# The seam between the mlp and attention: four copy buffers, passing products, bank sets by order of release, and a first turn without row maxima

## The chip, the cores and the metric

The kernel runs on one core of a Trainium2 chip. The metric is device time in microseconds (us). TensorE (PE) multiplies, VectorE (DVE), ScalarE (ACT) and GpSimd (POOL) work element by element, SyncE (SP) issues most of the transfers.

## The reference

Input x is 2048 x 448, all in float32. Two branches are mixed by a gate per token:

```
g = sigmoid((x * gate_w).sum(-1))
a = softmax(q k^T * 28**-0.5) v  per head (16 heads of 28), then @ wo      # q, k, v = x @ wqkv
b = gelu(layernorm(x) @ w1 + b1) @ w2 + b2                                   # 448 -> 1792 -> 448
out = g * a + (1 - g) * b
```

## The kernel before

Each float32 factor is split into a high part (rounded to fp32r, the matmul's one-pass type) and a low part (the rest), and a product is made of three: high by high, high by low, low by high.

The work has two stages. In the first (class `Strips`), PE is used as four strips of 32 rows; each strip has its own stream of small matmuls. A planner in Python (`Strips.run`, with estimated costs and ready times) writes their order out: first q, k and v (`QK`, `Val`), then the mlp in four chunks of 512 tokens: 14 tiles of w1 with the gelu (`Up`), then four tiles of w2 (`Down`, one of 128 tokens each). A piece collects in one of the PSUM banks 0 to 5; when its last strip is done, `close` empties the bank. For `Down` that is a copy by ACT into a buffer `gb` (L381, L382; two buffers) and a DMA issued from ACT's own queue to `gbs` in DRAM (L385). `st.free[bank]` holds the planner's estimate of the time at which a bank comes free.

Between these pieces, in both stages, run the row maxima of attention: a product of 128 queries with 512 keys in high precision only (L199), and a reduction on DVE (L201). 1024 of them are needed in all, kept in banks 6 and 7 in the first stage. Their results, by way of DRAM (`ms`), become a 29th row of the queries, so that the exp needs no further shift. They must be ready before the 64 units of a chunk that uses them.

The second stage is attention. Its unit is one head's 128 keys by 512 queries; there are 1024 units, 64 to each pair of a head group and a chunk of queries. A turn (`turn_of`) makes the scores of five units while row maxima are owed, and of six later. The turn's first three units go to banks 0, 1, 2 and the other two or three to banks 3, 4 (5): three passes of products each (L1108), then one exp of ACT over the bank set (L1111, tiles `p0` and `p1`). Turns of five units slip in three row maxima (`lone`), by way of banks 6, 5 and 6, turns of six up to two. Behind the scores stand the products of probabilities and values for all units of earlier turns, four at a time (`batch`, L1119, bank 7). In turn 0 there are none yet, and six products of the keys with themselves, whose result nobody reads, stand in their place (L1135, bank 7).

PE's order is exactly the order of the code. ACT, DVE, POOL and SP have each their own stream, in the order of the code; semaphores join the streams.

At the seam, the last four `Down` tiles (chunk 3) lie in banks 5, 1, 3 and 0, and are closed in that order. Attention's first scores, of turn 0, follow them on PE, with one maximum ahead of them. These scores need banks 0, 1 and 2.

Of the kernel before, what the change touches and what calls it, by code (L numbers as in the profile page):

```python
# [7 lines left out]
F32 = mybir.dt.float32  # L8
F32R = mybir.dt.float32r
AF = mybir.ActivationFunctionType  # L10
# [5 lines left out]
P = 128  # L16
S = 2048
D = 448
# [4 lines left out]
CH = 512  # L23
NC = S // CH
# [5 lines left out]
SCALE = DH ** -0.5  # L30
# [5 lines left out]
def kernel(ctx: ExitStack, tc: tile.TileContext, xt, wqk, wv, wo, xk, w1, b1, w2, b2,  # L36
                          ident_d, sel_d, out):
    nc = tc.nc
# [35 lines left out]
    bk = banks.tile([P, 8, CH], F32, name="bk")  # L74
# [87 lines left out]
    class RowMax:  # L162
# [51 lines left out]
        def close(self, n):  # L214
            mf, mt = self.mf[n % 2], self.mt[n % 2]
            nc.vector.reduce_max(mf[:, 0:16], self.mx[n % 2].rearrange("p j i k -> p (j i) k"), axis=AX)
            nc.vector.transpose(mt, mf)
# [17 lines left out]
    mhp = []  # L235
# [120 lines left out]
    class Down(Piece):  # L356
# [21 lines left out]
            return st.hready.get((self.c, f, p), 1e9) > now or self.c == 0 and st.w2ready.get(f, 1e9) > now  # L378

        def close(self, st, now):  # L380
            gb = mhp[0].tile([P, D], F32, name="gb", bufs=2)  # L381
            nc.scalar.activation(gb, bk[:, self.bank, :D], AF.Copy)  # L382
            st.use("act", now + 0.2, 0.56)
            st.free[self.bank] = st.act + 0.1
            nc.scalar.dma_start(gbs[self.c * TPC + self.i], gb)  # L385
            st.use("act", now, 0.5)

    class Strips:
# [28 lines left out]
        def at(self, t, fn, **uses):  # L417
            self.tasks.append((t, self.count, fn, uses))
            self.count += 1
# [358 lines left out]
    khi, klo, vg = {}, {}, {}  # L778
# [73 lines left out]
    strips = Strips([])  # L852
# [3 lines left out]
    for i, key in enumerate(load):  # L856
        r = slots[i % 8]
# [43 lines left out]
    m1.close()  # L901
    loads[0] = nc.sync


    def sb(name, bufs):
        return ctx.enter_context(tc.tile_pool(name=name, bufs=bufs, reuse_waits="tile"))
# [45 lines left out]
    def products(po, tt, groups):  # L952
        c, i = divmod(tt, TPC)
        sl = slice(i * P, (i + 1) * P)
        for g in groups:
            h, l = (t[:, g, sl] for t in ohs[c])
            nc.tensor.matmul(po, h, woh[:, g], start=(g == 0), stop=False, skip_group_check=True)  # L957
            nc.tensor.matmul(po, h, wol[:, g], start=False, stop=False, skip_group_check=True)  # L958
            nc.tensor.matmul(po, l, woh[:, g], start=False, stop=(g == NG - 1), skip_group_check=True)  # L959
# [7 lines left out]
    def project(tt):  # L967
        po = bk[:, 6, :D]
        products(po, tt, range(NG))
        put(po, tt)  # L970
# [60 lines left out]
    def begun(n, turn):  # L1031

        g, c = divmod(n, NC)
        if n + 1 < NG * NC:
            for j in range(4):
                at(turn + 1 + j // 2, lambda j=j: fetch_qq(n + 1, j))
            at(turn + 5, lambda: split_qq(n + 1))
            at(turn + 7, lambda: load_ms(n + 1))
        if c == (0 if g == 0 else 2) and g < NG - 1:
            for j in range(4):  # L1040
                at(turn + 2 + j, lambda j=j: fetch_kk(g + 1, j))
                at(turn + 8 + j, lambda j=j: split_kk(g + 1, j))
            at(turn + 13, lambda: key_row(g + 1))
            for t in range(2):
                at(turn + 9 + t, lambda t=t: load_v(g + 1, slice(8 * t, 8 * t + 8)))
        if g == NG - 1:
            for i in range(TPC):
                at(turn + 7 + i, lambda i=i: fetch_acc(c, i))
                at(turn + 9 + i // 2, lambda i=i: weigh_acc(c, i))
            for x in range(NG - 1):  # L1050
                at(turn + 4 + x, lambda x=x: split_o(x, c, ot[x][:, c * CH:(c + 1) * CH]))
# [14 lines left out]
    UNITS = NG * NC * 64  # L1066
    prob, tail = {}, []
    begins = set()
    cold = [0] * 4

    def lone(s, b, turn):
        if not rowmax.ready(s) or turn < cold[s]:
            return
        for kind, n, j in rowmax.one(s, bk[:, b]):
            if kind == "q":
                at(turn + 1, lambda n=n, j=j: rowmax.load_q(n, j))
            elif kind == "k":
                at(turn + 1, lambda n=n, j=j: rowmax.load_k(n, j))
                cold[j] = turn + 4
            else:  # L1080
                at(turn + 1, lambda n=n: rowmax.close(n))
                at(turn + 2, lambda n=n: rowmax.store(n))

    def turn_of(u, turn):

        left = UNITS - u
        owed = rowmax.left()
        size = min(left, 5 if owed and owed > 2 * ((left - 116) // 6) else 6)
        na, nb = min(3, size), max(0, size - 3)
        for x in range(u, u + size):  # L1090
            n = x // 64
            if n not in begins:
                begins.add(n)
                begun(n, turn)
        extra = {5: ((0, 3, 6), (3, 1, 5), (5, 2, 6)), 6: ((0, 3, 6), (5, 2, 6))}.get(size, ())
        for half, first, count in ((0, 0, na), (1, 3, nb)):
            for p in range(3):
                for x, o, b in extra:
                    if x == 3 * half + p:
                        lone((u + o) % 4, b, turn)  # L1100
                for i in range(first, first + count):
                    n, k = divmod(u + i, 64)
                    k, j = divmod(k, 4)
                    r = slice(32 * j, 32 * j + DH + (p == 0))
                    ks = slice(k * P, (k + 1) * P)
                    w = (khi, klo, khi)[p][n // NC]
                    q = (qh, qh, ql)[p][n % 3]
                    nc.tensor.matmul(bk[:, i], w[r, ks], q[r], start=(p == 0), stop=(p == 2), skip_group_check=True)  # L1108
            if count:
                t = ap.tile([P, 3, CH], F32, name=f"p{half}")  # L1110
                nc.scalar.activation(t[:, :count], bk[:, first:first + count], AF.Exp, scale=SCALE)  # L1111
                for i in range(count):
                    prob[u + first + i] = t[:, i]
        return size

    def batch(b, turn):
        n, k = divmod(b, NT)
        for j in range(4):
            nc.tensor.matmul(bk[32 * j:32 * j + 32, 7], vg[n // NC][:, k, 32 * j:32 * j + 32], prob.pop(4 * b + j),  # L1119
                             start=(k == 0), stop=(k == NT - 1), skip_group_check=True)  # L1120
        if k == NT - 1:
            valued(n, turn)
            return True
        return False

    u = b = turn = 0
    while b < UNITS // 4:
        before = u
        if u < UNITS:
            u += turn_of(u, turn)  # L1130
        for fn in agenda.pop(turn, ()):
            fn()
        if turn == 0:
            for _ in range(6):
                nc.tensor.matmul(bk[:, 7], khi[0][:, 0:P], khi[0][:, 0:CH], start=True, stop=True)  # L1135
        if before == UNITS:
            products(bk[:, 6, :D], (NC - 1) * TPC, range(NG - 1))
            before = u = UNITS
        while 4 * b + 4 <= before:
            b += 1  # L1140
            if batch(b - 1, turn):
                break
        if tail and tail[0][0] <= turn:
            project(tail.pop(0)[1])
        turn += 1
# [53 lines left out]
```

## Time and profile before

| | us |
|---|---|
| median of three runs | 1098.76 (1096.95 to 1099.1) |
| the profiled execution | 1098.27 |
| its span, first to last instruction | 1096.2 |
| PE busy | 1078.5 (98%) |
| DVE, ACT, POOL busy | 740.3, 634.5, 363.5 |
| mean granted clock of TensorE | 0.995 |

The page gives busy time and instructions of each engine; the span in 40 slices (the digits are tenths of busy time, for PEclk tenths of the full clock); the chain of work that ended last; and groups of instructions by line. In a timeline a row is: start, duration, engine, line, operation, what it writes and reads, how many; in brackets the idle time of the engine ahead of it and what ended that. "ACTq" and "SPq" are the issue of a DMA by that engine. A table of windows gives for each stretch its length, the busy time of each engine with its instructions in brackets, the granted clock, and the DMA engines' share and rate. In the chain of waits a row is start, duration and what.

### The profile page before, as it was taken

What the parts mean: (1) busy time and instruction counts of PE and PEld (TensorE: products, weight loads), DVE (VectorE), ACT (ScalarE), POOL (GpSimd) and SP (SyncE); (2) the same over time, 40 slices, a digit from 0 to 9 for tenths busy, and PEclk for the clock granted to TensorE, in tenths of its full rate; (3) what the DMA queues carried; (4) which work ended last, traced back from release to release, by engine and by line L of the source; (5) the groups of instructions that cost most, each with busy time, mean ns of one, the idle gap of its engine ahead of it and who ended that gap; (6) DMA issues with size and microseconds to landing.
All of it is one profiled execution on the core that took longest, in us unless ns stands there. A gap on an engine that the chain in (4) does not pass through costs nothing.

```text
span 1096.2 us, 30487 instructions
## 1 busy us (share of the span) xinstructions
PE 1078.5 (98%) x13166; PEld 726.3 (66%) x13166; DVE 740.3 (68%) x1186; ACT 634.5 (58%) x668; POOL 363.5 (33%) x372
## 2 busy tenths in 40 slices
PE   9999999999999999999999999999999999999998
PEld 7999999999999989544444444444444444454555
DVE  4289889999999998667766766567667666320102
ACT  5334471141250250478878878878878878857671
POOL 3547687245152166501100100310011215245431
PEclk9999999999999999899999999999999999999999
DMA  6795543104100105501000000500002101011111
GB/s 230 215 312 185 167 123 97 42 4 103 40 7 11 41 8 126 149 9 27 18 17 16 23 23 17 125 16 14 20 21 63 45 16 54 25 51 38 60 53 59
DMA packets 47462, 73.15 MB, mean 67 GB/s; under 512 B 13632, under 2 KB 28608, under 8 KB 46416
## 3 DMA queue, kind: packets, MB, share of 16 engines
q1 hardware_dynamic: 33888, 39.11, 12.9%
q0 software_dynamic: 4800, 16.89, 5.3%
q10 hardware_dynamic: 8640, 15.21, 3.9%
q8 instruction: 103, 1.69, 0.6%
q14 instruction: 31, 0.25, 0.1%
HBM read 51.75 MB, written 19.31 MB: 65 GB/s over the span
## 4 chain that ended last, share of the span: by engine, by line
PE 92%; ACT 3%; DVE 2%; issue 1%; DMA 1%; POOL 0%; SPq 0%; DVEq 0%; ACTq 0%; POOLq 0%
PE bk L472 33%; PE bk L1119 22%; PE bk L1108 18%; PE bk L199 15%; ACT p L1111 2%; PE bk L957 1%; PE bk L958 1%; PE bk L959 1%; DVE mx L201 1%; PE bk L883 1%; DMA first<-in_xt 0%; DMA gbs<-gb 0%; PE bk L1135 0%; ACT gb L382 0%; POOL hl L350 0%
## 5 line engine op out<-in xcount | busy, mean ns | idle before, releaser
L201 DVE TENSOR_REDUCE mx<-bk 128x1 f32<-128x512 f32 x1024 | 672.1, 688 | 203.7 <-PE bk L199 164.7
L1111 ACT ACTIVATE p<-bk 128x1536 f32<-128x1536 f32 (+1 forms) x395 | 481.7, 1275 | 147.4 <-PE bk L1108 147.4
L199 PE MATMUL bk<-kd,qd 28*128 28x512 f32 x1024 | 446.7, 439 | 3.3 <-DVE mx L201 1.8
L199 PEld LDWEIGHTS bk<-kd,qd 28*128 28x128 f32 x1024 | 186.4, 182 | 197.0 <-DVE mx L201 130.5
L472 PE MATMUL bk<-yh,w1f 32*128 32x512 f32 x1568 | 183.4, 392 | 0.4 <-ACT gb L382 0.4
L472 PE MATMUL bk<-yl,w1f 32*128 32x512 f32 x784 | 161.0, 391 | 0.0
L472 PEld LDWEIGHTS bk<-yh,w1f 32*128 32x128 f32 x1568 | 150.8, 183 | 2.3 <-ACT gb L382 1.7
L472 PE MATMUL bk<-w2h,hh 32*128 32x448 f32 x896 | 133.2, 366 | 1.3 <-ACT hh L343 1.3
L472 PE MATMUL bk<-w2l,hh 32*128 32x448 f32 x896 | 132.5, 363 | 0.0
L1119 PE MATMUL bk<-p,va 128*32 128x512 f32 x1024 | 132.1, 606 | 0.0
L1119 PE MATMUL bk<-p,vb 128*32 128x512 f32 x1024 | 129.5, 601 | 0.0
L350 POOL TENSOR_TENSOR hl<-h,hh 128x512 fp32r<-128x512 f32 x56 | 73.6, 1324 | 131.6 <-ACT hh L343 71.1
L1108 PE MATMUL bk<-yh,ka 29*128 29x512 f32 x512 | 108.4, 487 | 1.8 <-ACT gb L382 1.8
L803 POOL CAST yh<-yl 128x512 fp32r<-128x512 f32 x16 | 9.8, 610 | 298.0 <-DMA yl<-qk 219.6
L472 PEld LDWEIGHTS bk<-yl,w1f 32*128 32x128 f32 x784 | 103.3, 183 | 0.2
L1108 PE MATMUL bk<-yh,kb 29*128 29x512 f32 x512 | 98.4, 477 | 3.7 <-ACT p L1111 3.7
L472 PEld LDWEIGHTS bk<-w2h,hh 32*128 32x128 f32 x896 | 99.1, 183 | 1.8 <-ACT hh L343 1.7
L472 PEld LDWEIGHTS bk<-w2l,hh 32*128 32x128 f32 x896 | 99.9, 183 | 0.2
L1108 PE MATMUL bk<-yh,la 28*128 28x512 f32 x512 | 90.0, 397 | 0.0
L382 ACT ACTIVATE gb<-bk 128x448 f32<-128x448 f32 x16 | 8.7, 544 | 139.0 <-PE bk L472 134.2
L1108 PE MATMUL bk<-yl,ka 28*128 28x512 f32 x512 | 88.7, 413 | 0.0
L472 PE MATMUL bk<-w2h,hl 32*128 32x448 f32 x896 | 87.5, 362 | 0.0
(140 smaller groups left out, 1595.1 us busy)
## 6 DMA issues: line engine op xcount, KB each, us to landing
qk<-qo ACTq DMA_DIRECT2D x28, 256.0 KB
raw<-in_xt SPq DMA_DIRECT2D x17, 256.0 KB
vs<-vt ACTq DMA_DIRECT2D x16, 256.0 KB
rc<-rls SPq DMA_DIRECT2D x60, 64.0 KB
bxr<-in_xk POOLq DMA_DIRECT2D x8, 448.0 KB, 6.2
gbs<-gb ACTq DMA_DIRECT2D x16, 224.0 KB
acc<-gbs SPq DMA_DIRECT2D x16, 224.0 KB
out_y<-acc SPq DMA_DIRECT2D x16, 224.0 KB
```

The lines of the kernel that those rows point to most:

```text
L199: nc.tensor.matmul(ps, self.qd[n % 2][r, i * P:(i + 1) * P], self.kd[r, k * 512:(k + 1) * 512], start=True, stop=True)
L201: nc.vector.reduce_max(self.mx[n % 2][:, j, i, k:k + 1], ps, axis=AX)
L350: nc.gpsimd.tensor_sub(hl[f], h, hh[f].bitcast(F32))
L472: mm = nc.tensor.matmul(bk[:, x.bank, :n], a, b, start=x.first, stop=(len(x.rem) == 1 and m == len(ops) - 1), skip_group_check=True)
L803: nc.gpsimd.tensor_copy(h, l.bitcast(F32))
L883: nc.tensor.matmul(bk[:, b], w, v, start=(i == 0), stop=(i == len(ops) - 1), skip_group_check=True)
L957: nc.tensor.matmul(po, h, woh[:, g], start=(g == 0), stop=False, skip_group_check=True)
L958: nc.tensor.matmul(po, h, wol[:, g], start=False, stop=False, skip_group_check=True)
L959: nc.tensor.matmul(po, l, woh[:, g], start=False, stop=(g == NG - 1), skip_group_check=True)
L1108: nc.tensor.matmul(bk[:, i], w[r, ks], q[r], start=(p == 0), stop=(p == 2), skip_group_check=True)
L1111: nc.scalar.activation(t[:, :count], bk[:, first:first + count], AF.Exp, scale=SCALE)
L1119: nc.tensor.matmul(bk[32 * j:32 * j + 32, 7], vg[n // NC][:, k, 32 * j:32 * j + 32], prob.pop(4 * b + j), start=(k == 0), stop=(k == NT - ...
```

## The change

Four edits at the seam:

- The third and fourth of the last four `Down` tiles are copied to two buffers of the name `h` (those of the gelu, last used by the mlp's last `Up` tiles) instead of waiting for the two of `gb`.
- `shift` chooses, by the planner's estimates, which half of the banks 0 to 5 is free first; turns then use the sets in that order (`turn_bank`). Here the first set becomes banks 3, 4, 5 and the second 0, 1, 2, for all turns. The maxima that went to bank 5 go to bank 2.
- `idle` writes four products of the keys with themselves (nobody reads them) into the bank that has been free longest, bank 2, between the last mlp product and the first scores. The six of turn 0 stay.
- `cold = [1] * 4`: turn 0 makes no row maxima.

```diff
         def close(self, st, now):
-            gb = mhp[0].tile([P, D], F32, name="gb", bufs=2)
+            if self.c == NC - 1 and self.i > 1:
+                gb = mhp[0].tile([P, CH], F32, name="h", bufs=2)[:, :D]
+            else:
+                gb = mhp[0].tile([P, D], F32, name="gb", bufs=2)
             nc.scalar.activation(gb, bk[:, self.bank, :D], AF.Copy)
...
+    shift = min((0, 3), key=lambda o: max(strips.free[o + i] for i in range(3)))
+
+    def turn_bank(i):
+        return (i + shift) % 6
+
+    def idle(n, b):
+        for _ in range(n):
+            nc.tensor.matmul(bk[:, b], khi[0][:, 0:P], khi[0][:, 0:CH], start=True, stop=True)
+
+    idle(4, min(range(6), key=lambda b: strips.free[b]))
...
-    cold = [0] * 4
+    cold = [1] * 4
...
-                        lone((u + o) % 4, b, turn)
+                        lone((u + o) % 4, b if b == 6 else turn_bank(b), turn)
...
-                    nc.tensor.matmul(bk[:, i], w[r, ks], q[r], start=(p == 0), stop=(p == 2), skip_group_check=True)
+                    nc.tensor.matmul(bk[:, turn_bank(i)], w[r, ks], q[r], start=(p == 0), stop=(p == 2), skip_group_check=True)
...
-                nc.scalar.activation(t[:, :count], bk[:, first:first + count], AF.Exp, scale=SCALE)
+                b = turn_bank(first)
+                nc.scalar.activation(t[:, :count], bk[:, b:b + count], AF.Exp, scale=SCALE)
...
         if turn == 0:
-            for _ in range(6):
-                nc.tensor.matmul(bk[:, 7], khi[0][:, 0:P], khi[0][:, 0:CH], start=True, stop=True)
+            idle(6, 7)
```

What the change moves is seen in the order of the instructions. On PE, before the change, from the last `Down` products (L472) over turn 0 to the start of turn 1:

```order
L199 MATMUL bk<-kd,qd_150 128x512
L472 MATMUL bk<-w2h_3668,hl_2824 128x448
L199 MATMUL bk<-kd,qd_150 128x512
L1108 MATMUL bk<-yh,ka 128x512 x3
L1108 MATMUL bk<-yh,la 128x512 x3
L1108 MATMUL bk<-yl,ka 128x512 x3
L199 MATMUL bk<-kd,qd_150 128x512
L1108 MATMUL bk<-yh,ka 128x512 x2
L1108 MATMUL bk<-yh,la 128x512 x2
L199 MATMUL bk<-kd,qd_150 128x512
L1108 MATMUL bk<-yl,ka 128x512 x2
L1135 MATMUL bk<-ka 128x512 x6
```

The same place on PE after the change (its lines are 3 to 14 higher; L1121 is the scores, L914 the products of `idle`):

```order
L199 MATMUL bk<-kd,qd_150 128x512
L475 MATMUL bk<-w2h_3668,hl_2824 128x448
L914 MATMUL bk<-ka 128x512 x4
L1121 MATMUL bk<-yh,ka 128x512 x3
L1121 MATMUL bk<-yh,la 128x512 x3
L1121 MATMUL bk<-yl,ka 128x512 x3
L1121 MATMUL bk<-yh,ka 128x512 x2
L1121 MATMUL bk<-yh,la 128x512 x2
L1121 MATMUL bk<-yl,ka 128x512 x2
L914 MATMUL bk<-ka 128x512 x6
```

The four passing products took the place of turn 0's first maximum, and the two others are gone from between the scores. On ACT, before the change, the last four copies of `Down` with their DMA issues, and the first exps:

```order
L382 ACTIVATE gb_9624<-bk_115 128x448
L385 DMA gbs_90<-gb_9624 128x448
L382 ACTIVATE gb_9630<-bk_115 128x448
L385 DMA gbs_90<-gb_9630 128x448
L382 ACTIVATE gb_9639<-bk_115 128x448
L385 DMA gbs_90<-gb_9639 128x448
L382 ACTIVATE gb_9647<-bk_115 128x448
L385 DMA gbs_90<-gb_9647 128x448
L1111 ACTIVATE p0_9677<-bk_115 128x1536
```

And after it:

```order
L385 ACTIVATE gb_9624<-bk_115 128x448
L388 DMA gbs_90<-gb_9624 128x448
L385 ACTIVATE gb_9630<-bk_115 128x448
L388 DMA gbs_90<-gb_9630 128x448
L385 ACTIVATE h_9639<-bk_115 128x448
L388 DMA gbs_90<-h_9639 128x448
L385 ACTIVATE h_9647<-bk_115 128x448
L388 DMA gbs_90<-h_9647 128x448
L1125 ACTIVATE p0_9679<-bk_115 128x1536
```

The order is the same; only the third and fourth copy write another buffer. Since turn 0 makes no maxima, the later turns make them: before, 159 turns have five units, 38 have six, and the last has one; after, 161 have five, 36 have six, and the last has three. The number of turns stays 198.

## The prediction

> **What bounds the kernel now.** I read the page's busy shares first, then its row of the granted TensorE clock, then the chain.
>
> ```profile
> PE 1078.5 (98%) x13166; PEld 726.3 (66%) x13166; DVE 740.3 (68%) x1186; ACT 634.5 (58%) x668; POOL 363.5 (33%) x372
> ...
> PEclk9999999999999999899999999999999999999999
> ...
> PE bk L472 33%; PE bk L1119 22%; PE bk L1108 18%; PE bk L199 15%; ACT p L1111 2%; PE bk L957 1%; PE bk L958 1%; PE bk L959 1%; DVE mx L201 1%; PE bk L883 1%; DMA first<-in_xt 0%; DMA gbs<-gb 0%; PE bk L1135 0%; ACT gb L382 0%; POOL hl L350 0%
> ```
>
> TensorE is the bound: 1078.5 of 1096.2 us busy, and it fills the chain. So a gain must come from a stretch in which PE idles or runs slowly. The clock row has one dip, in the slice around 450 us, exactly where the mlp's last tiles give way to attention's first scores. I then cut that stretch into windows of 3.41 us, with one earlier thin window beside them.
>
> ```profile
> core 0: us, PE busy (x) PEld busy (x) DVE busy (x) ACT busy (x) POOL busy (x), PEclk, DMA share, GB/s
> 405.33:408.75 3.42, 2.10 (x43) 1.61 (x39) 2.38 (x4) 1.72 (x4) 3.12 (x3) 1.00 0.01 2
> 442.88:446.29 3.41, 2.85 (x44) 2.23 (x36) 3.34 (x6) 1.09 (x2) 1.73 (x3) 1.00 0.25 96
> 446.29:449.71 3.42, 1.44 (x16) 1.14 (x17) 0.87 (x2) 1.09 (x2) 1.58 (x2) 1.00 0.62 206
> 449.71:453.12 3.41, 3.41 (x14) 2.17 (x8) 1.29 (x2) 2.37 (x2) 0.00 (x0) 0.50 0.73 218
> 453.12:456.53 3.41, 3.41 (x21) 1.91 (x20) 1.44 (x3) 1.16 (x1) 2.34 (x4) 0.50 0.88 226
> 456.53:459.95 3.42, 3.42 (x23) 1.47 (x23) 1.23 (x2) 1.20 (x2) 3.34 (x4) 0.50 0.18 44
> 459.95:463.36 3.41, 3.41 (x36) 1.69 (x30) 2.43 (x4) 2.98 (x3) 3.25 (x5) 1.00 1.08 286
> ```
>
> The reader is to see two losses in one place. From 446.29 to 449.71 PE works only 1.44 of 3.42 us, 42%. Straight after it the granted clock is 0.50 for three windows, 10.24 us, although PE's rows are full; that is at most 10.24 x 0.5 = 5.1 us of lost PE time. A window with 2.10 of 3.42 us busy, 61%, at 405.33 drew no such answer. So the dip is bought somewhere between 42% and 61% of work in a window. The timeline shows why PE stood.
>
> ```profile
> 444.53 0.54 ACT L382 ACTIVATE gb<-bk 128x448 f32<-128x448 f32 x1 [34.39 <-PE bk L472]
> 445.11 0.33 ACTq L385 DMA_DIRECT2D gbs<-gb  x1
> ...
> 445.31 0.40 PE L472 MATMUL bk<-w2h,hl 32*128 32x448 f32 x1
> 445.54 0.54 ACT L382 ACTIVATE gb<-bk 128x448 f32<-128x448 f32 x1 [0.46 <-PE bk L472]
> 446.11 0.33 ACTq L385 DMA_DIRECT2D gbs<-gb  x1
> ...
> 446.52 0.50 PE L199 MATMUL bk<-kd,qd 28*128 28x512 f32 x1 [0.78 <-DVE mx L201]
> ...
> 447.13 0.54 ACT L382 ACTIVATE gb<-bk 128x448 f32<-128x448 f32 x1 [1.05 <-DMA gbs<-gb]
> 447.70 0.33 ACTq L385 DMA_DIRECT2D gbs<-gb  x1
> 448.13 0.54 ACT L382 ACTIVATE gb<-bk 128x448 f32<-128x448 f32 x1 [0.46 <-DMA gbs<-gb]
> 448.70 0.33 ACTq L385 DMA_DIRECT2D gbs<-gb  x1
> ...
> 448.77 0.65 PE L1108 MATMUL bk<-yh,ka 29*128 29x512 f32 x4 [1.75 <-ACT gb L382]
> ...
> 449.08 0.58 PE L1108 MATMUL bk<-yh,la 28*128 28x512 f32 x4
> ...
> 449.31 0.63 PE L1108 MATMUL bk<-yl,ka 28*128 28x512 f32 x4
> ```
>
> The last mlp product ends at 445.71. The third copy waits for a buffer (releaser: the DMA of the first copy). The first scores go to banks 0 to 2, bank 0 is emptied by the fourth copy, and PE starts them 0.10 us after that one's end (448.67 to 448.77). Each round of scores follows the one before by 0.23 us (449.08 to 449.31).
>
> **The change, part by part.** *Four buffers.* A copy follows the DMA issue ahead of it by 0.43 us when nothing is waited for (445.11 to 445.54). So copy three starts at 446.11 + 0.43 = 446.54 instead of 447.13 and ends at 447.08; its DMA is issued at 447.11, and copy four runs from 447.54 to 448.08, with its DMA issue at 448.11. The new buffers were last read by POOL's low parts (L350); the row of POOL is idle for 13.42 us until 444.48, so they are free.
>
> ```profile
> 444.48 0.56 POOL L928 CAST woh<-ob 128x448 fp32r<-128x448 f32 x1 [13.42 <-PE bk L472]
> ```
>
> *Bank sets.* The first set is now banks 3 to 5, whose last occupant is copy three; scores start at 447.08 + 0.10 = 447.18, which is 1.59 us sooner. The second half's banks wait for copy four, to 448.18, about when the first half's nine products have been issued.
>
> *Passing products.* Four full-height products go to an unused bank right behind the last mlp product, from about 445.55. A price is read from the six that stand there already, at half clock:
>
> ```profile
> 450.81 2.93 PE L1135 MATMUL bk<-ka 128*128 128x512 f32 x6
> ...
> 453.67 0.79 PE L199 MATMUL bk<-kd,qd 28*128 28x512 f32 x1
> ```
>
> That is 0.49 us each, 0.24 at full clock: four end near 446.5, before the scores may start. Their cover is the wait for copy three; without it they would cost 1.0 us. The idle stretch shrinks from 2.6 us (0.81 + 1.75, around the lone L199) to about 0.7, and the window from 446.29 to 449.71 then holds about 2.7 of 3.4 us, 80%, above the 61% that passed. **I take the clock to stay at 1.00.**
>
> Here a rule can be weighed. The Trainium skill, "TensorE: Matmul & The Clock Gate", section "Why this matters for your kernels", says to avoid idle gaps above about 3 us between bursts. By it the gaps here (0.81 and 1.75 us) are harmless, the dip has another cause and stays, and the change brings 1.6 us alone; that ends where the first rival below does. The trace disagrees so far, with 0.50 granted right behind the thin window. The same page, section "What's actually happening", has one busy window of about 3.4 us bring the clock back; by it a dip would cost 1.7 us, as the second rival's shortest does, but here three windows of full PE rows passed first.
>
> *The first turn without maxima.* Turn 0 has nine scores, then six; at full clock the first exp follows the first score by 1.04 us (448.77 to 449.81, below). So it is ready at 448.22, but ScalarE is free only 0.43 us after its last DMA issue: 448.54. It ends at 449.99. The second half's six scores run two side by side, three rounds of 0.23 us, 448.18 to about 448.9; six passing products follow to 448.9 + 6 x 0.24 = 450.3. Turn 1 starts there instead of at 453.67, and banks 3 to 5 are free. Its exp starts at 450.3 + 1.05 = 451.35. From there I go by the exps:
>
> ```profile
> 449.81 2.37 ACT L1111 ACTIVATE p<-bk 128x1536 f32<-128x1536 f32 x2 [1.14 <-PE bk L1108]
> 455.37 2.37 ACT L1111 ACTIVATE p<-bk 128x1536 f32<-128x1536 f32 x2 [3.19 <-PE bk L1108]
> 460.09 2.37 ACT L1111 ACTIVATE p<-bk 128x1536 f32<-128x1536 f32 x2 [2.35 <-PE bk L1108]
> 462.74 2.37 ACT L1111 ACTIVATE p<-bk 128x1536 f32<-128x1536 f32 x2 [0.29 <-PE bk L1108]
> 465.50 2.37 ACT L1111 ACTIVATE p<-bk 128x1536 f32<-128x1536 f32 x2 [0.38 <-PE bk L1108]
> 469.06 2.37 ACT L1111 ACTIVATE p<-bk 128x1536 f32<-128x1536 f32 x2 [1.20 <-PE bk L1108]
> ```
>
> Before, turns 0, 1, 2 are 5.56 and 4.72 us apart, then 2.65, 2.76, 3.56 (the last with two batches of value products). Now turns 1 to 5 come at 451.35, 454.06 (taking 2.71 for a turn with one batch), 456.7, 459.5 and 463.06. **The gain at turn 5 is 469.06 - 463.06 = 6.0 us.** It lies between 1.59 (clock drops all the same) and 1.59 + 5.1 = 6.7 (every half-speed microsecond was pure loss).
>
> *The three deferred maxima.* They are spread over later turns. By the order, turns stay 198, but 161 instead of 159 have five units, and the last turn has three instead of one. Rows for what this is worth:
>
> ```profile
> 466.19 1.85 PE bk L1119 x16
> 477.87 1.86 PE bk L1119 x16
> ...
> 1045.08 1.85 PE bk L1119 x16
> ...
> 1051.75 1.86 PE bk L1119 x16
> ```
>
> Four turns of five units take 11.68 us, a pair 5.84 with 2.5 batches; a pair of sixes takes 6.67 with three, so 6.67 - 0.46 (half a batch; sixteen rows are two batches in 1.85) = 6.21 against 5.84. Two sixes that become fives save at most 0.4 us. Against it stand three maxima of 0.23 us, 0.7 us if nothing ran beside them. Between -0.4 and +0.7 I take 0, since each shares PE with scores on other rows of the array. The last turn's exp grows from 0.60 us to the 1.45 of three banks:
>
> ```profile
> 1077.22 0.60 ACT L1111 ACTIVATE p<-bk 128x512 f32<-128x512 f32 x1 [3.26 <-PE bk L1108]
> ...
> 1080.08 1.06 PE L1119 MATMUL bk<-p,vb 128*32 128x512 f32 x8
> ```
>
> Its user starts at 1080.08 and 1077.22 + 1.45 = 1078.67, so it stays covered, with 1.4 us to spare.
>
> The profiled execution took 1098.27 us, 2.1 of them outside its span. **1098.27 - 6.0 = 1092.3 us.** That execution is 0.5 us under the median of the three runs, 1098.76; they spread by 2.1.
>
> **The rivals.** *The clock drops anyway* (passing products and strips of 28 rows may count for less than their rows suggest): only the earlier start stays, 1098.27 - 1.59 = 1096.7. The same time follows if the dip has another cause than the thin window. For it: PE's rows were full in the dip and the clock still took three windows. Against it: the window at 405.33, of row strips alone, passed at 61%.
>
> *A shorter dip*: one or two half-speed windows, 1.7 us each, give 1094.0 or 1095.7.
>
> *Slower: the clock drops and stays down longer.* The six passing products, full height, stood inside the dip before; now they lie ahead of it, and turn 1 onward offers mostly strips of 28 or 29 rows. If full-height work is what brings the clock back, each further window costs 1.7 us: 1098.4 after four, 1100.1 after five, so it is slower than before from the fifth window, 1101.8 after six. Against it: the dip ended at 459.95 with one batch in its window, and batches come with every turn from turn 1.
>
> *The change doesn't do what it says*: copy three still waits (for the POOL reader of its buffer, or a DMA). Then scores start at 447.67 + 0.10 = 447.77, and the rest holds: 1092.9.
>
> **How the numbers follow.** Clock stays: 0.79, and with a still waiting copy 0.02 more. Shorter dip 0.05. Full dip 0.10. Slower 0.04. The range starts at 1090.2 (the forecast less 0.4 for the sixes, less the 1.8 us by which the lowest run before lies under the median, rounded) and goes to 1095.7, the two-window dip; the full dip and the slower case stay outside, 0.14. About 0.2% of the median, 2.2 us, is what a measurement of this kernel can tell from no change, so faster means under 1096.6: the first three cases and about a third of the full dip, 0.89; same 0.07; slower 0.04.
>
> **What would show it.** In the changed kernel's profile: no slice of the clock row under 9 around 450 us; copies three and four about 1.0 us apart behind the second, with no DMA named as releaser; the first scores 1.5 us behind the last mlp product's end (3.06 before); exps of turns 0 and 1 under 3 us apart. If the clock still reads 0.50 there, the window's share of work is not what governs it. If the gain at turn 5 is 6 us and the end shows less, the deferred maxima or the sixes cost what I took as nothing.

## The result and the profile after

The changed kernel takes 1093.16 us (median of 4 runs, 1092.16 to 1093.73) against 1098.93 (4 runs, 1096.95 to 1099.74): ratio 0.9949, 95% interval 0.9932 to 0.9966. Measured again with the experiments it was 1094.30 (6 runs) against 1099.53 (13 runs), ratio 0.9955, interval 0.9940 to 0.9971. The profiled execution took 1093.73 us, 4.54 less than that of before; the prediction was 1092.3.

First the page of the changed kernel: busy shares and the granted clock.

```profile
PE 1074.6 (98%) x13170; PEld 724.8 (66%) x13170; DVE 739.2 (68%) x1186; ACT 634.8 (58%) x668; POOL 364.1 (33%) x372
...
PEclk9999999999999999999999999999999999999999
```

The reader is to see that the dip near 450 us is gone, and that PE is busy 3.9 us less although it makes four products more: at half clock the same products are longer. Three windows at the seam, cut as those of before:

```profile
442.87:446.28 3.41, 3.41 (x61) 3.08 (x56) 3.31 (x6) 0.54 (x1) 0.79 (x2) 1.00 0.32 101
446.28:449.69 3.41, 3.09 (x22) 1.71 (x21) 1.10 (x2) 1.89 (x4) 2.55 (x3) 1.00 0.57 200
449.69:453.11 3.42, 3.42 (x28) 2.19 (x24) 1.00 (x2) 2.64 (x3) 0.00 (x0) 1.00 0.49 168
```

PE works 3.09 of 3.41 us where it worked 1.44, and the next window runs at 1.00. The timeline of the changed kernel's seam (L475 and L385 are before's L472 and L382, L914 the passing products, L1121 the scores, L1125 the exps):

```profile
445.45 0.54 ACT L385 ACTIVATE gb<-bk 128x448 f32<-128x448 f32 x1 [34.25 <-PE bk L475]
...
446.45 0.55 ACT L385 ACTIVATE gb<-bk 128x448 f32<-128x448 f32 x1 [0.46 <-PE bk L475]
446.58 1.20 PE L914 MATMUL bk<-ka 128*128 128x512 f32 x4
...
447.46 0.55 ACT L385 ACTIVATE h<-bk 128x448 f32<-128x448 f32 x1 [0.46 <-POOL wol L942]
...
448.06 0.50 PE L1121 MATMUL bk<-yh,ka 29*128 29x512 f32 x3 [0.28 <-ACT h L385]
...
448.48 0.54 ACT L385 ACTIVATE h<-bk 128x448 f32<-128x448 f32 x1 [0.47 <-ACT h L385]
...
449.97 1.66 PE L914 MATMUL bk<-ka 128*128 128x512 f32 x6
...
451.56 0.50 PE L199 MATMUL bk<-kd,qd 28*128 28x512 f32 x1
```

The four copies are 1.0 us apart, no DMA is waited for, and PE idles 0.28 us ahead of the scores. Everything stands 0.92 us later than in before's profile already at the first copy (445.45 against 444.53), in code that the change doesn't touch. So below I measure from the start of the first of the four copies. The exps of turns 0 to 5 of the changed kernel:

```profile
449.44 2.37 ACT L1125 ACTIVATE p<-bk 128x1536 f32<-128x1536 f32 x2 [0.42 <-PE bk L1121]
452.58 2.37 ACT L1125 ACTIVATE p<-bk 128x1536 f32<-128x1536 f32 x2 [0.78 <-PE bk L1121]
455.30 2.37 ACT L1125 ACTIVATE p<-bk 128x1536 f32<-128x1536 f32 x2 [0.35 <-PE bk L1121]
458.07 2.37 ACT L1125 ACTIVATE p<-bk 128x1536 f32<-128x1536 f32 x2 [0.40 <-PE bk L1121]
460.77 2.37 ACT L1125 ACTIVATE p<-bk 128x1536 f32<-128x1536 f32 x2 [0.33 <-PE bk L1121]
464.34 2.37 ACT L1125 ACTIVATE p<-bk 128x1536 f32<-128x1536 f32 x2 [1.21 <-PE bk L1121]
```

| from the first copy, us | before | changed |
|---|---|---|
| first score | 4.24 | 2.61 |
| exp of turn 0 | 5.28 | 3.99 |
| exp of turn 1 | 10.84 | 7.13 |
| exp of turn 5 ("the distance") | 24.53 | 18.89 |
| end of the span | 651.7 | 646.2 |

The seam gives 5.64 us, 5.5 of it are left at the end, and 5.5 less the 0.92 lost ahead of the seam is the 4.5 between the two profiled executions.

### The profile page after: what moved, and what is told of

Same layout as the page of the kernel before. It is cut to its first block, busy times and chain, and to the rows that moved or that the text cites. A ratio compares the mean times of both kernels' runs of the same rounds, so it can differ in the third digit from the quotient of the medians.

```text
span 1091.6 us, 30496 instructions
## 1 busy us (share of the span) xinstructions
PE 1074.6 (98%) x13170; PEld 724.8 (66%) x13170; DVE 739.2 (68%) x1186; ACT 634.8 (58%) x668; POOL 364.1 (33%) x372
## 4 chain that ended last, share of the span: by engine, by line
PE 93%; ACT 2%; DVE 2%; issue 1%; DMA 1%; POOL 0%; DVEq 0%; ACTq 0%
PE bk L475 33%; PE bk L1133 22%; PE bk L1121 18%; PE bk L199 15%; ACT p L1125 2%; PE bk L970 1%; DVE mx L201 1%; PE bk L971 1%; PE bk L972 1%; PE bk L886 1%; DMA qk<-qo 1%; PE bk L871 0%; DVE ob L992 0%; POOL hl L350 0%; DVE acc L977 0%
## 5 line engine op out<-in xcount | busy, mean ns | idle before, releaser
L1125 ACT ACTIVATE p<-bk 128x1536 f32<-128x1536 f32 (+1 forms) x395 | 482.1, 1276 | 142.2 <-PE bk L1121 142.2
L475 PE MATMUL bk<-yh,w1f 32*128 32x512 f32 x1568 | 183.0, 391 | 0.4 <-ACT gb L385 0.4
L475 PE MATMUL bk<-yl,w1f 32*128 32x512 f32 x784 | 161.0, 391 | 0.0
L475 PEld LDWEIGHTS bk<-yh,w1f 32*128 32x128 f32 x1568 | 151.8, 183 | 2.2 <-ACT gb L385 1.7
L475 PE MATMUL bk<-w2h,hh 32*128 32x448 f32 x896 | 133.2, 366 | 1.3 <-ACT hh L343 1.3
L475 PE MATMUL bk<-w2l,hh 32*128 32x448 f32 x896 | 132.5, 363 | 0.0
L1121 PE MATMUL bk<-yh,ka 29*128 29x512 f32 x512 | 107.0, 482 | 0.3 <-ACT h L385 0.3
L475 PEld LDWEIGHTS bk<-yl,w1f 32*128 32x128 f32 x784 | 103.6, 183 | 0.2
L1121 PE MATMUL bk<-yh,kb 29*128 29x512 f32 x512 | 98.1, 477 | 3.8 <-ACT p L1125 3.5
L475 PEld LDWEIGHTS bk<-w2h,hh 32*128 32x128 f32 x896 | 99.5, 183 | 1.9 <-ACT hh L343 1.7
L475 PEld LDWEIGHTS bk<-w2l,hh 32*128 32x128 f32 x896 | 100.4, 183 | 0.1
L1121 PE MATMUL bk<-yh,la 28*128 28x512 f32 x512 | 88.5, 393 | 0.0
L385 ACT ACTIVATE gb<-bk 128x448 f32<-128x448 f32 x14 | 7.6, 545 | 138.3 <-PE bk L475 133.3
L475 PE MATMUL bk<-w2h,hl 32*128 32x448 f32 x896 | 87.3, 362 | 0.0
L1121 PE MATMUL bk<-yl,ka 28*128 28x512 f32 x512 | 86.9, 410 | 0.0
```

The lines of the kernel that those rows point to most:

```text
L475: mm = nc.tensor.matmul(bk[:, x.bank, :n], a, b, start=x.first, stop=(len(x.rem) == 1 and m == len(ops) - 1), skip_group_check=True)
L1121: nc.tensor.matmul(bk[:, turn_bank(i)], w[r, ks], q[r], start=(p == 0), stop=(p == 2), skip_group_check=True)
L1125: nc.scalar.activation(t[:, :count], bk[:, b:b + count], AF.Exp, scale=SCALE)
```

## The experiments

Two theories stood at first: that the share of time in which PE works in a 3.4 us window governs the clock, and that the early start alone counts. The clock of each execution is given as its mean over the span; the changed kernel had 0.999 to 1.000 in nine of ten, since up to 3.2 us at the end of a profiled span, behind the last products, are at 0.50.

**Passing products alone.** The kernel before with eleven of them:

```diff
     loads[0] = nc.sync
+    for _ in range(11):
+        nc.tensor.matmul(bk[:, 2], khi[0][:, 0:P], khi[0][:, 0:CH], start=True, stop=True)
```

> The kernel before, with eleven passing products (keys by keys, bank 2, nobody reads them) between the last mlp product and attention's first scores; buffers, bank sets and maxima as before. They keep TensorE at work until about when the fourth copy ends, so the start of the scores stays where it was. Measured from the start of the first of the four last copies to the exp of turn 5, before takes 24.53 us and the changed kernel 18.89. Theory (the share of work in a 3.4 us window governs the clock): granted clock 1.00 throughout the seam, that distance 20.3 to 21.0 us, total about 1095. Rival (the dip has another cause, and only the earlier start of the scores counts): clock 0.50 for about 10 us, distance 24.5, total as before, 1098.9.

Measured: distance 20.16 us, just under the 20.3 expected, the clock 1.00 throughout the seam, total 1095.64 (7 runs) against 1098.98 (16 runs), ratio 0.9971 (0.9956 to 0.9985). The first copy, the exp of turn 5, and two windows at the seam:

```profile
446.10 0.55 ACT L382 ACTIVATE gb<-bk 128x448 f32<-128x448 f32 x1 [34.08 <-PE bk L472]
...
466.26 2.37 ACT L1112 ACTIVATE p<-bk 128x1536 f32<-128x1536 f32 x2 [1.19 <-PE bk L1109]
...
445.08:448.50 3.42, 3.42 (x38) 2.65 (x31) 2.88 (x5) 1.09 (x2) 2.28 (x4) 1.00 0.27 100
448.50:451.91 3.41, 3.41 (x26) 2.28 (x24) 1.00 (x2) 1.66 (x3) 1.07 (x1) 1.00 0.67 235
```

The scores started where they did before (4.20 us behind the first copy against 4.24), so 24.53 - 20.16 = 4.4 of the 5.6 us are the clock's. The rival falls.

**The change without its passing products.**

```diff
-    idle(4, min(range(6), key=lambda b: strips.free[b]))
```

> The changed kernel without the four passing products ahead of the first scores. TensorE then idles about 1.4 us there; a 3.4 us window around it still holds some 58% of work, between the 42% that was followed by the dip and the 61% that was not. Theory (share of work in a window, nearer to 61): clock stays at 1.00, distance from the first copy to the exp of turn 5 stays at 18.9 us, total 1093. Rival (any idle stretch of over 1 us between the stages drops the clock, so the passing products are what carries the gain): clock 0.50 for three windows, distance up to 18.9 + 4.4 = 23.3, total up to 1097.5.

Measured: 1099.13 us (10 runs, mean clocks 0.994 to 0.998) against 1098.98, ratio 0.9998 (0.9981 to 1.0015): in the total nothing is seen of the gain. The distance in its profile is 21.50 us, 2.6 more than the changed kernel's and 3.0 less than before's, and the dip is two windows:

```profile
448.13 0.54 ACT L385 ACTIVATE gb<-bk 128x448 f32<-128x448 f32 x1 [34.19 <-PE bk L199]
...
469.63 2.37 ACT L1124 ACTIVATE p<-bk 128x1536 f32<-128x1536 f32 x2 [1.19 <-PE bk L1120]
...
447.76:451.17 3.41, 1.96 (x26) 1.36 (x21) 2.29 (x4) 1.65 (x4) 2.93 (x4) 1.00 0.36 133
451.17:454.59 3.42, 3.42 (x18) 2.14 (x13) 0.00 (x0) 2.89 (x3) 0.39 (x1) 0.50 0.69 199
454.59:458.00 3.41, 3.41 (x20) 2.28 (x20) 0.69 (x1) 0.12 (x1) 0.00 (x0) 0.50 0.23 56
458.00:461.41 3.41, 3.41 (x36) 1.62 (x37) 2.57 (x4) 3.06 (x3) 1.86 (x3) 1.00 0.97 267
```

I expected no dip after 58% of work; a window with 1.96 of 3.41 us, 57%, was followed by one. The mean clocks, 0.998 at most, suggest a dip in all ten runs. The early start by itself doesn't show in the totals, but their interval, from 2.1 us faster to 1.6 slower, doesn't exclude the 1.6 us that it was forecast to bring.

The profiled execution took 1098.98 us, 0.71 more than that of before, although its seam is 3.0 us shorter: its first copy stands at 448.13 against 444.53. About half of that delay comes from the start of the run, where the code is the same (the second product on 64 rows starts at 14.26 us here, at 12.42 in before). A stretch there, in this profile and then in before's:

```profile
5.98:10.80 4.82, 4.82 (x11) 3.51 (x12) 3.21 (x5) 4.28 (x7) 1.77 (x3) 1.00 1.01 363
5.98:10.80 4.82, 4.45 (x16) 2.62 (x17) 2.08 (x4) 3.67 (x7) 1.31 (x3) 1.00 1.03 367
```

Without the products, full-height matmuls follow each other by 0.43 us there until 10.7 us (7.27, 7.70, 8.13); in before they follow by 0.23 from 6.2 us on. The clock column reads 1.00 in both, but the trace's record of the clock begins only at 10.85 and at 5.97 us. So a single profile's total mixes what the seam costs with how the run began, and the mean clocks don't count the beginning.

**Two buffers.** The changed kernel with all four copies in `gb`:

```diff
-            if self.c == NC - 1 and self.i > 1:
-                gb = mhp[0].tile([P, CH], F32, name="h", bufs=2)[:, :D]
-            else:
-                gb = mhp[0].tile([P, D], F32, name="gb", bufs=2)
+            gb = mhp[0].tile([P, D], F32, name="gb", bufs=2)
```

> The changed kernel with the third and fourth copy back in the two gb buffers. The third copy then waits for the DMA of the first, 2.60 us after the first copy's start instead of 2.01. Theory: the first scores come 0.6 us later, the clock stays at 1.00, the distance from first copy to the exp of turn 5 is 19.4 to 19.5 us, total about 1093.7. Rival (the start of turn 1 is set by the exps and the six passing products of turn 0, so that 0.6 us ahead of them is absorbed): 18.9 us.

Measured: distance 19.46 us, no dip, as the theory had it: the two more buffers are worth 0.6 us at the seam. In the total, 1093.33 (4 runs), ratio 0.9948 (0.9929 to 0.9968), that cannot be seen.

**Bank sets in the old order.**

```diff
-    shift = min((0, 3), key=lambda o: max(strips.free[o + i] for i in range(3)))
+    shift = 0
```

> The changed kernel with the bank sets in the old order (banks 0 to 2 first). The first scores wait for the fourth copy's end, 3.57 + 0.10 us after the first copy's start instead of 2.61; the second half then waits for nothing. Theory: turn 1 starts 0.9 to 1.0 us later, distance to the exp of turn 5 19.8 us, clock 1.00, total about 1094.1. Rival (ScalarE's last DMA issue and the first exp bound the start of turn 1 anyway): 18.9 to 19.1 us.

Measured: distance 21.06, 1.3 more than expected, since the clock did dip, for one window; total 1095.41 (4 runs, mean clocks 0.997 and 0.998), ratio 0.9963 (0.9948 to 0.9977).

```profile
445.69:449.11 3.42, 2.10 (x18) 1.26 (x16) 0.18 (x1) 1.59 (x3) 1.61 (x2) 1.00 0.63 210
449.11:452.52 3.41, 3.41 (x11) 2.33 (x14) 0.00 (x0) 1.86 (x2) 0.00 (x0) 0.50 0.44 128
452.52:455.93 3.41, 3.41 (x39) 1.81 (x35) 2.44 (x4) 2.37 (x2) 0.56 (x1) 1.00 0.67 184
```

This broke the first theory. 2.10 us of work were followed by a dip here; the same 2.10 us at 405.33 in the kernel before were not. What differs is the number of products: that window shows 43, this one 18. So a new theory, below called A: what counts is how much of the array works, and a product on 32 rows counts a quarter of one on 128. The first theory, that PE's busy time counts, is called B.

**Four passing products on 32 rows.** The changed kernel with:

```diff
-    idle(4, min(range(6), key=lambda b: strips.free[b]))
+    for _ in range(4):
+        nc.tensor.matmul(bk[:, 2], khi[0][0:32, 0:P], khi[0][0:32, 0:CH], start=True, stop=True)
```

> The changed kernel with its four passing products ahead of the first scores cut to 32 of the 128 rows (same count, columns and bank). TensorE's rows in the trace are then as busy as in the changed kernel. Theory A (what governs the clock is the share of the array's rows that work, summed over a 3.4 us window): the seam's window falls from about 0.46 of the array to about 0.28, the clock goes to 0.50 for one to three windows in most runs, distance from first copy to the exp of turn 5 20.5 to 23.5 us in the profile, median total 1097 to 1099, as without the products. Theory B (the share of time in which TensorE works at all, as the prediction had it): clock 1.00, distance 18.9, total 1093.2.

Measured: distance 18.88, no dip at the seam, 1094.80 (7 runs, mean clocks 0.997 to 0.999), ratio 0.9951 (0.9936 to 0.9966). This is what theory B expected, and A's total of 1097 to 1099 is missed. But in the profile the windows fell so that the thin stretch was cut in two, 32 products having started in the window up to 450.31, so it doesn't decide between the two; how often a window can fall so is estimated below the table of windows. The same profile has a dip elsewhere, in the mlp:

```profile
262.57:265.99 3.42, 1.36 (x29) 1.01 (x25) 1.43 (x3) 0.00 (x0) 0.00 (x0) 1.00 0.99 209
265.99:269.40 3.41, 3.41 (x38) 3.33 (x41) 1.82 (x3) 0.00 (x0) 1.12 (x1) 0.50 0.67 199
```

**Eleven on 32 rows.** To take the chance out, the first experiment with its eleven products cut to 32 rows (and put into bank 4 instead of 2), so that PE never idles and yet most of the array does:

```diff
     loads[0] = nc.sync
+    for _ in range(11):
+        nc.tensor.matmul(bk[:, 4], khi[0][0:32, 0:P], khi[0][0:32, 0:CH], start=True, stop=True)
```

> The kernel before with eleven passing products ahead of the first scores, as in the first experiment, but on 32 of the 128 rows (and into bank 4). TensorE's rows in the trace have no idle time at the seam then; the share of the array that works falls to about 0.2 in the thinnest 3.4 us window, where windows of 0.22 to 0.29 were followed by a dip so far and windows from 0.33 up were not. Theory A (share of the array): the clock dips at the seam in most runs, distance from first copy to the exp of turn 5 22 to 25 us, median total 1097.5 to 1099.5. Theory B (share of time in which TensorE works at all): no dip at the seam, distance 20.2, total 1095.6, as with the full-height products.

Measured: distance 22.67 us, total 1097.65 (10 runs, mean clocks 0.994 to 0.998) against 1098.21 (13 runs), ratio 0.9986 (0.9975 to 0.9997).

```profile
447.70:451.11 3.41, 3.41 (x30) 2.68 (x23) 2.31 (x4) 1.53 (x3) 2.91 (x4) 1.00 0.36 132
451.11:454.53 3.42, 3.42 (x20) 2.37 (x19) 0.77 (x2) 1.18 (x3) 0.43 (x1) 0.50 0.63 203
454.53:457.94 3.41, 3.41 (x8) 1.82 (x6) 1.21 (x2) 1.83 (x2) 0.00 (x0) 0.50 0.22 54
457.94:461.35 3.41, 3.41 (x37) 1.79 (x37) 2.11 (x4) 2.34 (x2) 1.91 (x3) 1.00 0.94 263
```

PE is busy 3.41 of 3.41 us, and the clock halves straight after. The mean clocks of the ten runs say the same: none is above 0.998, where the seven of the first experiment lie at 0.997 to 1.000. Theory B falls; theory A holds.

**Maxima in turn 0 again.**

```diff
-    cold = [1] * 4
+    cold = [0] * 4
```

> The changed kernel with row maxima in turn 0 again (three of them, between the scores). Theory: they run beside the scores on other rows of the array and cost turn 1's start under 0.2 us; three maxima fewer are left for later turns, worth nothing either way; distance 18.9 to 19.1 us, clock 1.00, total within 0.5 us of the changed kernel's 1093.2. Rival (the deferral is a gain of its own: the first maximum stands ahead of the first scores, and the second half of the turn gets a third round): distance 19.4 or more, total 1093.7 to 1094.2.

Measured: distance 18.88, as without them; the end comes 646.5 us after the first copy against 646.0 of the changed kernel on the same chip; total 1094.56 (4 runs) against its 1094.30, ratios 0.9956 (0.9942 to 0.9969) and 0.9955. The deferral brings nothing at the seam and is worth at most some 0.5 us later. This profile has a thin window that passed, in the mlp:

```profile
262.18:265.60 3.42, 1.74 (x34) 1.35 (x27) 1.92 (x3) 0.00 (x0) 0.00 (x0) 1.00 0.99 189
```

**Fewer products behind turn 0**, and beside it the changed kernel once more:

```diff
-            idle(6, 7)
+            idle(2, 7)
```

> The changed kernel with two instead of six passing products behind turn 0's scores; the four ahead of them stay. In the changed kernel the six end at 451.56 us, while the exp that turn 1's scores wait for ends at 450.89. Theory: turn 1's scores start 0.5 us sooner, distance 18.3 to 18.4 us, the window's share of the array stays above 0.4 and the clock at 1.00, total 1092.6. Rival (the thinner window drops the clock as the missing products ahead of the scores did): clock 0.50 for a window or more, total 1094.5 to 1098.

> The changed kernel itself, beside the other three on the same chip. Every theory: distance 18.9 us, clock 1.00 at the seam, total 1093.2, and the same ratio to before as in its first measurement, 0.995.

Measured: distance 18.36 against 18.87, as the theory had it, the end 0.66 us nearer to the first copy (645.35 against 646.01). In the totals, 1094.51 against 1094.30 (6 runs each; ratios 0.9956 and 0.9955), half a microsecond is lost in the spread of 3 to 5 us. It may be a better kernel; it is not shown to be.

**Fourteen products in turn 0 of the kernel before**, to see what ends a dip:

```diff
-            for _ in range(6):
+            for _ in range(14):
                 nc.tensor.matmul(bk[:, 7], khi[0][:, 0:P], khi[0][:, 0:CH], start=True, stop=True)
```

> The kernel before with fourteen instead of six passing products behind turn 0's scores, so that a whole half-speed window is filled with full-height work. So far the clock came back after windows with 0.41 to 0.57 of the array at work and not after 0.31 to 0.40. Theory A: a window full of them (0.5 at half clock) brings the clock back, so the dip is two windows, 6.8 us, instead of three; distance 25.4 us, since eight more products cost more than the window saves. Rival (a dip lasts three windows whatever runs in it): 10.2 us at 0.50, distance 26.5.

Measured: distance 24.97 for the 25.4 of theory A, two windows at 0.50 as it had them, total 1100.04 (10 runs) against 1098.95, ratio 1.0006 (0.9991 to 1.0021).

```profile
447.57:450.98 3.41, 1.12 (x6) 0.37 (x4) 2.05 (x4) 1.48 (x3) 2.76 (x3) 1.00 0.42 151
450.98:454.39 3.41, 3.15 (x18) 2.36 (x19) 0.97 (x2) 1.59 (x3) 0.00 (x0) 0.50 0.69 219
454.39:457.81 3.42, 3.42 (x9) 2.65 (x9) 0.32 (x1) 0.93 (x2) 0.00 (x0) 0.50 0.51 145
457.81:461.22 3.41, 3.41 (x29) 2.08 (x31) 1.47 (x3) 0.99 (x1) 2.97 (x4) 1.00 0.82 194
```

The clock came back after the window that held eight full-height products. Dips of one and two windows elsewhere speak against a fixed three as well.

**All windows together.** I count the products that start in a window in the timeline, one for a product on 28 to 32 rows and four for one on 128:

| window | PE busy, us | count | clock in the next |
|---|---|---|---|
| fourteen products, 447.57 | 1.12 | 4 | 0.50 |
| before, 446.29 | 1.44 | 16 | 0.50 |
| no products, 447.76 | 1.96 | 18 | 0.50 |
| old order, 445.69 | 2.10 | 19 | 0.50 |
| four on 32 rows, 262.57 | 1.36 | 21 | 0.50 |
| eleven on 32 rows, 447.70 | 3.41 | 22 | 0.50 |
| fewer in turn 0, 447.16 | 3.08 | 24 | 1.00 |
| maxima in turn 0, 262.18 | 1.74 | 27 | 1.00 |
| two buffers, 446.32 | 2.52 | 27 | 1.00 |
| changed, 446.28 | 3.09 | 31 | 1.00 |
| before, 405.33 | 2.10 | 36 | 1.00 |

The count parts these outcomes without a miss; busy time doesn't (3.41 dips, 1.74 passes). All other full-speed windows of the twelve profiles, from the start of the clock's record on, agree (value products counted as four), except that 24 stands on both sides: at the end of the run with eleven full-height products a window of 24 (1086.79, 1.56 us busy) kept the clock, and at the end of the run with fourteen a window of 24 (1092.69, 1.50 us busy) lost it. At one round of 0.23 us and four strips of the array a full window has room for some 59, so I estimate the border at near 40% of the array.

Half-speed windows follow about the same border, less cleanly: after 18, 21, 21 and 26 the clock stayed at 0.50, after 25, 28, 28, 32 and 34 it came back. Two windows of before are left out of this: 18 and two value products (stayed), 14 and six (came back). A value product works 128 rows but only 32 columns, and what it counts was not tested by itself; if it counted for nothing, every profile would have windows of 9 to 14 that kept the clock.

Since the windows fall anywhere, I laid them at every position over the seam of each profile and took the thinnest. The changed kernel has 30 to 39 there (in both its profiles), eleven full-height products 38 to 46, fewer in turn 0 24 to 35, two buffers 19 to 35, and four products on 32 rows 18 to 33, with 22 or fewer in 56% of the positions. By this estimate the changed kernel's seam doesn't depend on where the windows fall. The seam with four products on 32 rows does, which fits a median that shows the dip only in part: four of its seven mean clocks are 0.999.

## Why the prediction was right, and where it was not

- *Four buffers, bank sets:* right. The scores came 1.63 us sooner against 1.59 forecast, 0.6 of it by the buffers alone; the old order cost its 1.0 and a dip besides.
- *Passing products:* the outcome was right, the measure wrong. The step said that the window would hold "about 2.7 of 3.4 us, 80%, above the 61% that passed". It held 3.09, but that is not why the clock stayed: 57% and 61% were followed by dips in the experiments, and so was 100%. By the count, what held it is that each of the four products works all 128 rows; an experiment shows this for eleven products, not for these four. The doubt stood in the first rival ("strips of 28 rows may count for less than their rows suggest") and was argued away with the window at 405.33, whose 43 row strips were many, not thin.
- *The cover of the passing products:* right; they ended 0.28 us before the scores could start, not the 0.7 expected.
- *The first turn and the exps:* 5.64 us at turn 5 for 6.0. The exp of turn 0 gained 1.29 (1.27 forecast). Turn 1 started 1.59 us after the six passing products did, not 6 x 0.24 = 1.44, and the six scores ahead of them took 0.90, not 0.7. These two make the missing 0.35.
- *The deferred maxima:* taken as 0; putting them back cost nothing at the seam and about 0.5 us by the end, in one profile each.
- *The clock dips anyway* was nearer than its chance: without four products of 1.2 us the same kernel is not measurably faster than before.
- *The base:* the forecast took 6.0 from one execution. Of the 0.9 us by which the median lies above it, 0.35 is the seam's; the rest lies within the spread of the parts ahead of the seam (first copy at 443.9 to 448.1 us over all profiles).
- *The skill's rules:* the Trainium skill, "TensorE: Matmul & The Clock Gate", section "Why this matters for your kernels", says to avoid idle gaps above about 3 us, and the runs show that this is not enough: passing products in gaps of 0.81 and 1.75 us took the dip away, and a dip came with no gap at all. The other rule (section "What's actually happening"), one busy window brings the clock back, agrees if busy means about 25 of the count above; the three half-speed windows of before were 26, then 18 and 14 with two and six value products besides.

## What to carry to other kernels

A stage that ends on a few strips of the array can cost more after its end than in it: look for a granted clock of 0.50 behind a stretch with few products, not only behind idle rows. If real work cannot fill the stretch, a few full-height products that wait for nothing can; on strips of 32 rows they don't. And an early start that leaves the stretch thin may not show in the total, because the clock takes time back: here it cost 2.6 of the 5.6 us at the seam, in one profile.

## What the runs showed of the hardware that was not expected

The clock in a window of 3.41 us followed what the window before had held, at full and at half speed with about the same border (down after 22 quarter products and fewer, either way after 24, not after 27; back after 25 in one case and not after 26 in another). The windows run on regardless of the code: every dip was one, two or three times 3.41 us, all changes of the clock within a profile lie whole windows apart (130 of them from 5.97 to 449.71 us in before's), and the same code fell differently in them. The same kernel varies: over the sixteen runs beside the first experiments the kernel before took 1095.48 to 1101.11 us, with mean clocks of 0.993 to 0.998, and the kernel of four products on 32 rows lost a window at 266 us, in the mlp, which the other profiles did not. The start varies too: in two profiles (no products, eleven on 32 rows) the first full-height products stay 0.43 us apart until 10.7 us, in before's and the changed kernel's only until about 6. Whether the whole spread comes from all this is open.
